# Attention, MLP and gate in one program: the middle of the run follows a written-out order table

## The chip, the core and the metric

The program runs on one core of a Trainium2 chip. Five engines work side by side, each through its own queue of instructions in order: PE (TensorE, matrix products into PSUM), ACT (ScalarE, activations), DVE (VectorE), POOL (GpSimd) and SP (SyncE, here only starting transfers). PSUM has eight banks of 128x512 fp32; a matrix product writes a bank and ScalarE or VectorE must have read it before it is written again. Between engines a semaphore carries "this is done"; inside an engine the order of the queue is all there is.

The metric is the device time of one execution in microseconds (us). Three runs of the kernel before gave 664.42, 664.42 and 664.57.

## What is computed

The input is x (2048 rows of 512), with 32 query heads of width 16 over one shared key and value head, and an MLP of width 1792. Cut to what matters:

```
xn = layernorm(x)
q  = (xn @ wq) as 32 heads of 16;  k = xn @ wk;  v = xn @ wv
p  = softmax(q k^T / 4);  s = (p v, heads side by side) @ wo
g  = silu( silu(xn @ w1) @ w2 )
out = x + s * g
```

All tensors are bf16 outside of PSUM.

## The kernel before

**Planning.** The program isn't written down instruction by instruction. While it is built, a planner (class `Planner`, from L117 on) keeps a clock for each engine and a price for each kind of work (`T_P` for a VectorE pass, `T_P64` for a GpSimd shift, `MM` for a group of matmuls and so on, L36 to L55). The main loop at the end of the kernel takes the engine whose clock is furthest behind and lets its step function (`pe_step`, `act_step`, `generic_step`) place one more operation: an instruction, or a group of four matmuls. What comes out is one list for each engine; `finalize` adds the semaphore waits that the reads and writes of tiles need. The clocks only settle the order. On the chip nothing is left of them.

**Scores.** Work is cut into 32 passes (`NG`), each of which has 512 queries of four heads (i = 0 to 3), and every head has 16 blocks of 128 keys. One product of 128 keys x 16 dimensions by 512 queries fills one PSUM bank (L946). It uses a strip of 32 of PE's rows, so up to four of them, on four strips and into four banks, run at once: an S group (`do_S`, L1086 on). Two engines turn scores into exponentials:

- ScalarE's way ("a"): one `Exp` activation over one, two or three neighbouring banks into `pa_sb` (`act_step`, L1845).
- VectorE's way ("d"): `tensor_scalar` multiplies by 128 log2(e), adds a constant and writes uint16, which read as bf16 is a rough 2^x, into `db_sb` (L1082). Four of those form a batch. GpSimd then adds 32, 64 and 96 to all values of a batch, as packed 64-bit sums, into `ds_sb` (the shifts, L1291; `make_shifts`, `split`): the same exponentials at other places of the rounding pattern. The four versions with weights `SHIFT_W` average its error away. A shift can also be done by VectorE (L1285).

Both ways need PE again: the product with v is 32 columns wide, so four run at once on column strips, one for each head, and add up in bank 7: a C group (`do_pv`, L1371). A key block of ScalarE's way needs one such product, one of VectorE's way four (one from `db_sb`, three from `ds_sb`). Columns of ones in `v_sb` give the sums of the softmax in the same products.

**Other work on PE.** Jobs (`mk_q`, `mk_h`, `mk_z`, `mk_w`) are the projections and the MLP: some rounds each, a round being a C group (L577), with a bank of their own from start to eviction. A round can also be cut into four pieces of 32 rows (`piece`, L689); a piece fits into the free strip of an S group that has three score products. Job results go through ScalarE (`Tanh`, L740) and VectorE (L742), or VectorE alone (L699, L796).

**Normalisation.** When a pass is done, VectorE transposes bank 7 (L1427), takes reciprocals (L1430), multiplies (L1431, `otr_sb`) and, every second pass, transposes again (L1438).

**Who excludes whom.** Some VectorE instructions have two inputs in tiles, or read and write tiles only: `otr_sb` (L1431), `ob_sb` (L808), the shift on VectorE (L1285). The planner marks them with `ports=2`, as it does GpSimd's shifts, and never lets one of VectorE's and one of GpSimd's run at the same time: `place` makes each wait by semaphore for the last marked operation of the other engine (`last2`), and `avail` keeps a shift back if a marked VectorE task will be ready within `HOLD_PO`.

**What sets the order around the change.** `pe_step` chooses between an S group, a group with v and a job round by thresholds on queues and banks; `do_S` chooses how many products go which way and into which banks; `act_step` takes up to three finished scores in neighbouring banks; `generic_step` takes VectorE's and GpSimd's ready task of the best priority. Random numbers with fixed seeds (`SEEDS`, `redraw`, `vary`) vary these choices every eight S groups. The start (load, layer norm, first keys: the first `NPRO` jobs) and the end (`make_tail`: the last product with wo, the gate and the stores) have code of their own.

Of the kernel before, what the change touches and what calls it, by code (L numbers as in the profile page):

```python
# [15 lines left out]
P = 128  # L16
DH = 16
NQ = 512
# [31 lines left out]
K = len(SHIFT)  # L50
PH = []

PE, AC, DV, PO, SP = "PE", "ACT", "DVE", "POOL", "SP"
ENGINES = (PE, AC, DV, PO, SP)
MM = 216.0  # L55
BLG = 0
# [38 lines left out]


class Task:
    __slots__ = ("eng", "dur", "emit", "reads", "writes", "prio", "preds", "op", "on_place", "dma", "gate", "ports", "after", "ring", "first")

    def __init__(self, eng, dur, emit, reads=(), writes=(), prio=5, preds=(), on_place=None, dma=0, gate=None, ports=1):  # L100
        self.ports, self.after, self.ring = ports, None, None
# [210 lines left out]
def bass_recurrent_scan__grouped_kv_mqa__dense_activation_silu__prompt_kernel(  # L312
# [30 lines left out]
    with ExitStack() as es:  # L343
# [350 lines left out]
        def mk_q(oi):  # L694
            c, o = divmod(oi, NOC)

            def consume(jb, op):
                b = jb.bank
                t = Task(DV, T_P, lambda v: v.tensor_scalar(qt_sb[:, oi % NQR, :], bank(b), QSCALE, None, op0=ALU.mult),  # L699
                         [("ps", b)], [("qT", oi % NQR)], 0)  # L700
                q_done[oi] = t
# [31 lines left out]
        def gated(b, k, scale, dst, key, kind):  # L733
            src, held = bank(b), ("ps", b)
            t0 = None
            if kind in EVAC:
                src, held = hs_sb[:, k, :], ("hs", k)
                t0 = Task(DV, T_P, lambda v: v.tensor_copy(hs_sb[:, k, :], bank(b)), [("ps", b)], [held], 0,
                          [hs_last.get(k)])
            t1 = Task(AC, 490.0, lambda a: a.activation(t_sb[:, k, :], src, ACT.Tanh, scale=scale),  # L740
                      [held], [("t", k)], 0, [t0])
# [3 lines left out]
            t2.first = [t1, t2] if t0 is None else [t0]  # L745
            if t0 is not None:
                hs_last[k] = t2
                pl.add(t1)
                pl.add(t2)
            return t2  # L750
# [54 lines left out]
        def final(tt, b, r=None):  # L805
            t1 = scaled(tt, b, r)
            src, key = fin_of(tt, r)
            t2 = Task(DV, 333.0, lambda v: v.tensor_tensor(ob_sb[:, tt % 4, :], src, xr_sb[:, tt % 4, :], ALU.add),  # L808
                      [key, ("xr", tt % 4)], [("ob", tt % 4)], PR_OB if r is None else 1,
                      [t1, xr_task[tt], out_task.get(tt - 4)], ports=2)  # L810
            fin_task[tt], out_task[tt] = t2, store(tt, t2)
            return t1, t2

# [261 lines left out]
        def pass_d(b, bt, g, i, kt):  # L1075
            tot[g, i] += K

            def placed(pop):
                pool_free.append(b)
                pvq[g][i].append((pop, v_lhs(1, g, kt), db_sb[:, bt.b, i * NQ:(i + 1) * NQ].bitcast(BF16),  # L1080
                                  [("Db", bt.b, i)] + v_reads(1, kt), ("d", bt), None))
            bt.P[i] = pl.add(Task(DV, T_P, lambda v: v.tensor_scalar(  # L1082
                db_sb[:, bt.b, i * NQ:(i + 1) * NQ], bank(b), 128.0 * LOG2E, 128.0 * (SHIFT_BETA + 127.0),
                op0=ALU.mult, op1=ALU.add), [("ps", b)], [("Db", bt.b, i)], 0, on_place=placed))

        def do_S(t):  # L1086
            banks = [b for r, b in bank_times() if r <= t + 30][:4]
# [328 lines left out]
        def make_norm(g):  # L1416
# [6 lines left out]
            if g == NG - 1:  # L1423
# [9 lines left out]
                rcp_sb[:, k, :].unsqueeze(2).to_broadcast([P, NQ // 32, DH]), ALU.mult),  # L1433
                [("F", k), ("rcp", k)], [("otr", oi % 2, e)], PR_OTR, [t2, t2_task.get(oi - 2)], ports=2))
            norm[("m", g)] = t3
            if e == 1:
                cc = oi // NOC - NON // NOC
                t2_task[oi] = pl.add(Task(DV, T_TR, lambda v: v.transpose(on_sb[:, oi % NON, :], otr_sb[:, oi % 2, :]),  # L1438
                                          [("otr", oi % 2, 0), ("otr", oi % 2, 1)], [("on", oi % NON)], 4,
                                          [t3, norm[("m", g - 1)]],  # L1440
                                          gate=lambda: cc < 0 or all(tt in w_rounds for tt in range(4 * cc, 4 * cc + 4))))


        kt1 = {}
# [334 lines left out]
        def half_step(t):  # L1779
# [24 lines left out]
                st["halfdone"] = True  # L1804
            return True

        def act_step():
            t = pl.clk[AC]
            now, soon = pl.best(AC, t)
# [29 lines left out]
                pl.place_task(now[1])  # L1839
                return True  # L1840
            if rx is not None and rx <= t + 25:
                q.sort(key=lambda u: u.bank)
                b0, b1 = q[0].bank, q[-1].bank
                step = q[1].bank - b0 if n > 1 else 1
                op = pl.place(AC, 0.8333 * NQ * n + T_AF, lambda a: a.activation(  # L1845
                    pa_sb[:, s * NQ:(s + n) * NQ].rearrange("p (b n) -> p b n", n=NQ), ps3[:, b0:b1 + 1:step, :], ACT.Exp),
                    [("ps", u.bank) for u in q], [("pA", s + d) for d in range(n)])
                for d in range(n):
                    pa_busy[s + d] = 1
                st["expn"] += n  # L1850
                for k, u in enumerate(q):
                    g, i, kt = u.slot
                    pool_free.append(u.bank)
                    pvq[g][i].append((op, v_lhs(0, g, kt), pa_sb[:, (s + k) * NQ:(s + k + 1) * NQ],
                                      [("pA", s + k)] + v_reads(0, kt), ("a", s + k), None))
                return True
            if soon is not None:
                nxt = min(nxt, soon[2])
            if rx is not None:
# [3 lines left out]
        def generic_step(e):  # L1863
            t = pl.clk[e]
            now, soon = pl.best(e, t)
            if now is not None:
                pl.place_task(now[1])
                return True
            return soon[2] if soon is not None else INF

        steps = {PE: pe_step, AC: act_step, DV: lambda: generic_step(DV), PO: lambda: generic_step(PO),
                 SP: lambda: generic_step(SP)}
        idle = {e: -1.0 for e in ENGINES}
        while True:
            e = min(ENGINES, key=lambda e: pl.clk[e])
# [73 lines left out]
```

## Time and profile before

| | |
|---|---|
| median of three runs | 664.42 us |
| span of the profiled execution | 662.9 us |
| time around the span (median less span) | 1.5 us |
| PE, ScalarE, VectorE, GpSimd busy | 652.8, 652.0, 613.6, 564.8 us |
| score products / products with v | 2048 / 4272 |
| exponential activations of ScalarE | 689, and 4 over half-width pairs of banks at the end |
| exponential passes of VectorE | 740 |
| shifts on GpSimd / on VectorE | 548 / 7 |

The profile is of one execution, with start and length of each instruction. Lengths include the time until the result has landed, so instructions of one engine overlap in it: the step from one start to the next is shorter than the length, and it is the step that says how much an engine can do. Groups of instructions are named by the line of the kernel, the engine, the operation and the tiles (out<-in). An idle time stands with the instruction that ended it (releaser).

### The profile page before, as it was taken

What the parts mean: (1) busy time and instruction counts of PE and PEld (TensorE: products, weight loads), DVE (VectorE), ACT (ScalarE), POOL (GpSimd) and SP (SyncE); (2) the same over time, 40 slices, a digit from 0 to 9 for tenths busy, and PEclk for the clock granted to TensorE, in tenths of its full rate; (3) what the DMA queues carried; (4) which work ended last, traced back from release to release, by engine and by line L of the source; (5) the groups of instructions that cost most, each with busy time, mean ns of one, the idle gap of its engine ahead of it and who ended that gap; (6) DMA issues with size and microseconds to landing.
All of it is one profiled execution on the core that took longest, in us unless ns stands there. A gap on an engine that the chain in (4) does not pass through costs nothing.

```text
span 662.9 us, 21201 instructions
## 1 busy us (share of the span) xinstructions
PE 652.8 (98%) x8958; PEld 189.3 (29%) x8959; DVE 613.6 (93%) x1085; ACT 652.0 (98%) x786; POOL 564.8 (85%) x564
## 2 busy tenths in 40 slices
PE   8899999999999999999999999999999999999997
PEld 4332222222222222222222222222222222222222
DVE  8989999999999999999999999999999999998986
ACT  7999999999999999999999999999999999999996
POOL 3059999999997889998999889899999888979973
PEclk9999999999999999999999999999999999999999
DMA  9500000000000100000000000000000001000000
GB/s 303 167 9 2 2 2 2 2 2 2 1 2 18 34 18 2 1 2 2 2 2 1 18 18 18 18 2 1 2 2 2 2 18 33 2 18 2 2 2 33
DMA packets 11501, 12.86 MB, mean 19 GB/s; under 512 B 1808, under 2 KB 10768, under 8 KB 11408
## 3 DMA queue, kind: packets, MB, share of 16 engines
q1 hardware_dynamic: 10784, 10.65, 5.0%
q8 instruction: 72, 1.18, 0.8%
q0 software_dynamic: 192, 0.46, 0.2%
q10 hardware_dynamic: 432, 0.39, 0.2%
q14 instruction: 21, 0.17, 0.1%
HBM read 8.95 MB, written 2.10 MB: 17 GB/s over the span
## 4 chain that ended last, share of the span: by engine, by line
PE 90%; ACT 4%; DVE 4%; DMA 1%; issue 0%; SPq 0%; DVEq 0%
PE ps L1371 40%; PE ps L946 30%; PE ps L577 19%; ACT pa_sb L1845 4%; DMA ds_sb<-in_A_x_dram 1%; DVE stats_sb L488 1%; DVE db_sb L1082 1%; ACT t_sb L740 0%; PE ps L593 0%; SPq L423 0%; DVE xn_sb L520 0%; DVE ds_sb L1285 0%; DVE xnT_sb L606 0%; DVE fin_sb L796 0%; DVE f_sb L1395 0%
## 5 line engine op out<-in xcount | busy, mean ns | idle before, releaser
L1845 ACT ACTIVATE pa_sb<-ps 128x1024 bf16<-128x1024 f32 (+2 forms) x689 | 615.4, 1004 | 2.9 <-PE ps L946 2.0
L1291 POOL INT64_ADD ds_sb<-db_sb x548 | 556.8, 1038 | 57.9 <-DVE otr_sb L1431 31.6
L1082 DVE TENSOR_SCALAR db_sb<-ps 128x512 uint16<-128x512 f32 x740 | 476.4, 682 | 35.5 <-PE ps L946 20.6
L1371 PE MATMUL ps<-ds_sb,v_sb 128*32 128x512 bf16 x2220 | 265.2, 384 | 0.2 <-DVE ds_sb L1285 0.2
L946 PE MATMUL ps<-qt_sb,kt_sb 32*128 32x512 bf16 x2048 | 250.3, 385 | 3.7 <-ACT pa_sb L1845 1.5
L1371 PE MATMUL ps<-pa_sb,v_sb 128*32 128x512 bf16 x1312 | 231.6, 383 | 0.2 <-DVE var_sb L512 0.2
L1371 PE MATMUL ps<-db_sb,v_sb 128*32 128x512 bf16 x740 | 161.6, 384 | 0.0
L946 PEld LDWEIGHTS ps<-qt_sb,kt_sb 32*128 32x128 bf16 x2048 | 62.7, 91 | 274.6 <-ACT pa_sb L1845 149.7
L1371 PEld LDWEIGHTS ps<-ds_sb,v_sb 128*32 128x32 bf16 x2220 | 63.8, 95 | 62.1 <-issue 45.2
L577 PE MATMUL ps<-xnT_sb,w_sb 128*32 128x512 bf16 x896 | 71.1, 383 | 0.0
L1371 PEld LDWEIGHTS ps<-pa_sb,v_sb 128*32 128x32 bf16 x1312 | 57.0, 95 | 43.3 <-issue 31.0
L577 PE MATMUL ps<-w_sb,u_sb 128*32 128x512 bf16 x776 | 62.5, 383 | 0.0
L689 PE MATMUL ps<-w_sb,u_sb 32*128 32x512 bf16 x120 | 46.2, 385 | 0.0
L1371 PEld LDWEIGHTS ps<-db_sb,v_sb 128*32 128x32 bf16 x740 | 40.0, 95 | 20.2 <-issue 15.4
L740 ACT ACTIVATE t_sb<-ps 128x512 bf16<-128x512 f32 x72 | 45.1, 626 | 0.0
L742 DVE SCALAR_TENSOR_TENSOR u_sb<-t_sb,ps 128x512 bf16<-128x512 bf16 x56 | 38.2, 683 | 1.1 <-ACT t_sb L740 0.2
L577 PEld LDWEIGHTS ps<-xnT_sb,w_sb 128*32 128x32 bf16 x896 | 18.2, 95 | 24.1 <-issue 16.1
L1427 DVE STREAM_TRANSPOSE f_sb<-ps 128x512 f32<-128x512 f32 x31 | 21.9, 706 | 1.9 <-PE ps L1371 1.8
L1448 POOL DMA_DIRECT2D kt_sb<-kt_sb x4 | 2.3, 563 | 24.9 <-DVE kt_sb L638 14.7
L577 PEld LDWEIGHTS ps<-w_sb,u_sb 128*32 128x32 bf16 x776 | 15.4, 95 | 19.9 <-issue 17.0
L577 PE MATMUL ps<-wo_sb,on_sb 128*32 128x512 bf16 x256 | 19.3, 383 | 0.0
L577 PE MATMUL ps<-xnT_sb,wq_sb 128*32 128x512 bf16 x240 | 18.7, 383 | 0.0
(83 smaller groups left out, 180.9 us busy)
## 6 DMA issues: line engine op xcount, KB each, us to landing
w_sb<-in_B_w_dram SPq DMA_DIRECT2D x2, 1792.0 KB, 14.0
xr_sb<-in_A_x_dram SPq DMA_DIRECT2D x16, 128.0 KB, 2.4
out_dram<-ob_sb SPq DMA_DIRECT2D x15, 128.0 KB, 1.7
ds_sb<-in_A_x_dram SPq DMA_DIRECT2D x3, 512.0 KB, 6.9
wq_sb<-in_A_wq_dram SPq DMA_DIRECT2D x1, 512.0 KB, 5.0
wo_sb<-in_A_wo_dram SPq DMA_DIRECT2D x1, 512.0 KB, 16.3
kt_sb<-kt_sb POOLq DMA_DIRECT2D x4, 112.0 KB, 3.8
ds_sb<-in_A_x_dram SPq DMA_DIRECT2D x2, 128.0 KB, 2.8
```

What stands on the lines that cost most here:

```text
L488: ts_ = pl.add(Task(DV, 593.0, lambda v, t=t: v.bn_stats(stats_sb[:, t, :], x_tile(t)), [xkey(t)], [("st", t)], 1 + j, gate=(lambda j=j: S ...
L577: last = h.matmul(bank(b)[32 * j:32 * (j + 1), 0:n], lhsT=lhs(j), rhs=rhs, start=start, stop=stop, tile_position=(0, 32 * j), skip_group_c ...
L689: return (lambda pe: pe.matmul(bank(b), lhsT=lhs(k, rows, 0, P), rhs=rhs(k, rows), start=False, stop=last, tile_position=(32 * i, 0), skip ...
L740: t1 = Task(AC, 490.0, lambda a: a.activation(t_sb[:, k, :], src, ACT.Tanh, scale=scale), [held], [("t", k)], 0, [t0])
L742: t2 = Task(DV, T_P, lambda v: v.scalar_tensor_tensor(out=dst, in0=t_sb[:, k, :], scalar=1.0, in1=src, op0=ALU.add, op1=ALU.mult), [held, ...
L946: return pe.matmul(bank(b), lhsT=kt_sb[32 * i:32 * i + 32, g % 2, kt * P:(kt + 1) * P], rhs=qt_sb[32 * i:32 * i + 32, (g // 2) % NQR, :], ...
L1082: bt.P[i] = pl.add(Task(DV, T_P, lambda v: v.tensor_scalar(db_sb[:, bt.b, i * NQ:(i + 1) * NQ], bank(b), 128.0 * LOG2E, 128.0 * (SHIFT_BET ...
L1291: whole["po"].append(pl.add(Task(PO, T_P64, lambda g, cols=cols: g.int64_add(ds_sb[:, s, cols].bitcast(U64), db_sb[:, bt.b, cols].bitcast( ...
L1371: h = pe.matmul(bank(OB)[32 * i:32 * (i + 1), cols], lhsT=lhs, rhs=rhs, start=s0, stop=s1, tile_position=(0, 32 * i), skip_group_check=True)
L1427: t1 = pl.add(Task(DV, T_TR, lambda v: v.transpose(f_sb[:, k, :], bank(OB)), [("ps", OB)], [("F", k)], 1, [norm.get(("m", g - 2))]))
L1448: kt1[c] = pl.add(Task(PO, T_SWDGE, lambda e: e.dma_start(kt_sb[DH:P, 1, cols], kt_sb[0:P - DH, 0, cols]), [("kt0", k) for k in range(4 * ...
L1845: op = pl.place(AC, 0.8333 * NQ * n + T_AF, lambda a: a.activation(pa_sb[:, s * NQ:(s + n) * NQ].rearrange("p (b n) -> p b n", n=NQ), ps3[ ...
```

## The change

The choices of `pe_step`, `act_step` and `generic_step` in the middle of the run are replaced by a table, `ORDER`, which has one string for each of PE, ScalarE, VectorE and GpSimd. It begins to hold when the jobs of the start are placed and no task of theirs is left (`ordered`), and each engine goes back to its own step function when its string is used up. The strings read like this:

- PE: `S` is an S group: how many products go ScalarE's way, how many VectorE's, a character for each that names bank and head, and a strip for a job piece or `.`. `L` adds one product to the S group just placed, on a free strip. `P` is a group with v, with a letter for each head: `a`, `d` or `s` for the tile it takes (`pa_sb`, `db_sb`, `ds_sb`) or `-`. `N` starts a job in the bank given, `J` is a job's next round.
- ScalarE: a digit is an exponential over so many banks, `T` a Tanh.
- VectorE: a digit is the eviction of that bank into `db_sb`; letters are q, the gate's product, the steps of the normalisation and the last steps of an output (tags given to the tasks).
- GpSimd: the place in its list of waiting shifts, always the first.

Two prices of the planner change too: `T_P` from 600 to 598 and `T_P64` from 1035 to 1014. `place_exp` is the old code of `act_step`, moved into a function. Activations still read only neighbouring banks.

```diff
-T_P, T_SH, T_TR, T_AF = 600.0, 600.0, 630.0, 64.3
-T_P64, DV_MIN, T_LIB = 1035.0, 40, 300.0
+T_P, T_SH, T_TR, T_AF = 598.0, 600.0, 630.0, 64.3
+T_P64, DV_MIN, T_LIB = 1014.0, 40, 300.0
...
+S_WIDE = 3.0
+ORDER = {
+    PE: (
+        "S216CM.LdfPaaaaN0JS11Yu.LaNJJPaaaaS214Al.LdyPaddaS21N[,.PdaaaPssadS214Bk.N6JJJS21M[..PaassS21:Dm.PssssPssaaPa-ssS01-.S21"
...
+    AC: (
+        "1122222T22222T2T222221T2T22222222222T2T12222222322232221T221T222222T2T2222222322222222222222T22323232222222222222T222222"
...
+    DV: (
+        "356Q56050H506a262bHc6H54656156H1H45645645645646a6H1H5Q25265265b6c5d252H5465H6256256a5Hb6cH2623623635625625625656a56b5c6d"
...
+        def ordered():
+            if not at.get("on"):
+                at["on"] = st["pro"] >= NPRO and not active and x_free[0] and not any(pl.tasks[e] for e in (AC, DV, PO)) and (
+                    pl.clk[PE] <= min(pl.clk[e] for e in (AC, DV, PO)))
+            return at["on"]
...
+        def order_S(late):
+            if late:
+                nA, nD, codes, gap = (1, 0, next_of(PE, 3)[2], ".") if next_of(PE, 2)[1] == "a" else (0, 1, next_of(PE, 3)[2], ".")
+                size = 3
+            else:
+                nA, nD = int(next_of(PE, 2)[1]), int(next_of(PE, 3)[2])
+                size = 4 + nA + nD
+                codes, gap = next_of(PE, size)[3:-1], next_of(PE, size)[-1]
+            slots = [slot_of(ch, k >= nA) for k, ch in enumerate(codes)]
+            if any(b not in pool_free for b, _, _ in slots):
+                return INF
...
+            dur = MM + (S_WIDE if len(mm) + (pj is not None) > 3 else 0.0)
+            start = pl.order[PE][-1].t0 + 10.0 if late else pe_start(pl.clk[PE], "S")
+            op = pl.place(PE, dur, emit, sorted(set(reads), key=str), writes,
+                          t0=max(start, pl.ready(PE, reads, writes)), after=pj.prev if pj is not None else None)
...
+        def order_task(e, tag):
+            task = next((x for x in pl.tasks[e] if x.tag == tag), None)
+            if task is None or pl.avail(task) is None:
+                return INF
+            at[e] += 1
+            pl.place_task(task)
+            return True
+
+        def order_step(e):
+            if e == PE:
+                return order_pe()
+            c = next_of(e)
+            if e == PO:
+                if len(pl.tasks[PO]) <= int(c) or pl.avail(pl.tasks[PO][int(c)]) is None:
+                    return INF
+                at[e] += 1
+                pl.place_task(pl.tasks[PO][int(c)])
+                return True
+            if e == DV or c == "T":
+                return order_task(e, c)
+            n = int(c)
+            if len(units) - st["expn"] < n or place_exp(units[st["expn"]:st["expn"] + n], pl.clk[AC]) is None:
+                return INF
+            at[e] += 1
+            return True
+
+        def step_of(e, own):
+            def step():
+                if ORDER and e in ORDER and ordered() and at[e] < len(ORDER[e]):
+                    return order_step(e)
+                return own()
+            return step
+
         steps = {PE: pe_step, AC: act_step, DV: lambda: generic_step(DV), PO: lambda: generic_step(PO),
                  SP: lambda: generic_step(SP)}
+        steps = {e: step_of(e, fn) for e, fn in steps.items()}
```

`order_pe` (not shown) reads the next letter and calls `order_S`, or places the group with v or the job round that the letter names.

More of the change, by code (lines that the diff above doesn't have):

```diff
@@ L1805, in half_step, with place_exp @@
             return True
+        def place_exp(q, t):
+            n = len(q)
+            free = [k for k in range(NPA - n + 1) if not any(pa_busy[k:k + n])]
+            if not free:
+                return None
+            s = min(free, key=lambda k: max(pl.ready(AC, (), [("pA", k + d)]) for d in range(n)))
+            q = sorted(q, key=lambda u: u.bank)
+            b0, b1 = q[0].bank, q[-1].bank
+            step = q[1].bank - b0 if n > 1 else 1
+            op = pl.place(AC, 0.8333 * NQ * n + T_AF, lambda a: a.activation(
+                pa_sb[:, s * NQ:(s + n) * NQ].rearrange("p (b n) -> p b n", n=NQ), ps3[:, b0:b1 + 1:step, :], ACT.Exp),
+                [("ps", u.bank) for u in q], [("pA", s + d) for d in range(n)])
+            for d in range(n):
+                pa_busy[s + d] = 1
+            st["expn"] += n
+            for k, u in enumerate(q):
+                g, i, kt = u.slot
+                pool_free.append(u.bank)
+                pvq[g][i].append((op, v_lhs(0, g, kt), pa_sb[:, (s + k) * NQ:(s + k + 1) * NQ],
+                                  [("pA", s + k)] + v_reads(0, kt), ("a", s + k), None))
+            return True
         def act_step():
@@ L1841, in act_step @@
             if rx is not None and rx <= t + 25:
[L1842 to L1856, printed above, removed]
+                return place_exp(q, t)
             if soon is not None:
```

222 lines of the change are left out of this document (220 added, 2 removed).

## The prediction

> **What bounds the kernel now.** I read the page first: the busy shares, then the shares of the chain that ended last.
>
> ```profile
> span 662.9 us, 21201 instructions
> PE 652.8 (98%) x8958; PEld 189.3 (29%) x8959; DVE 613.6 (93%) x1085; ACT 652.0 (98%) x786; POOL 564.8 (85%) x564
> PE 90%; ACT 4%; DVE 4%; DMA 1%; issue 0%; SPq 0%; DVEq 0%
> ```
>
> Four engines are nearly full, but the chain lies on PE for 90%. A busy share can't say how full PE is, since a matmul's record is longer than the step to the next. The pieces of that chain, in order of time, give the price of PE's work (start, length, what):
>
> ```profile
> 644.95 1.19 PE ps L1371 x20
> 646.14 0.33 PE ps L946 x4
> 646.47 0.98 PE ps L1371 x16
> ```
>
> Matmuls go in groups of four that run at once, in two kinds: S groups (score products on row strips, L946, with a 32-row piece of a job, L689, in a free strip) and C groups (column strips: L1371, L577). Five C groups take 1.19 and four 0.98, so a C group costs 0.21 to 0.22 (0.216 below; the last digit is from start times); four cost 0.86, so 0.11 is left for the change of kind, and an S group lasts 0.33, 0.11 over a C group, for the change back. A pair of changes costs 0.22.
>
> The timeline of PE shows the same step by step, and the only waits in it (start, length, instruction):
>
> ```profile
> 61.36 0.60 PE L577 MATMUL ps<-xnT_sb,w_sb 128*32 128x512 bf16 x8
> 61.94 0.39 PE L946 MATMUL ps<-qt_sb,kt_sb 32*128 32x512 bf16 x3
> ...
> 302.37 0.39 PE L946 MATMUL ps<-qt_sb,kt_sb 32*128 32x512 bf16 x3
> 302.38 0.38 PE L689 MATMUL ps<-w_sb,u_sb 32*128 32x512 bf16 x1
> 302.70 0.62 PE L1371 MATMUL ps<-ds_sb,v_sb 128*32 128x512 bf16 x8
> 303.25 0.39 PE L946 MATMUL ps<-qt_sb,kt_sb 32*128 32x512 bf16 x3
> ...
> 637.66 0.62 PE L1371 MATMUL ps<-ds_sb,v_sb 128*32 128x512 bf16 x8
> 638.26 0.39 PE L946 MATMUL ps<-qt_sb,kt_sb 32*128 32x512 bf16 x3
> ...
> 636.92 1.88 DVE L1082 TENSOR_SCALAR db_sb<-ps 128x512 uint16<-128x512 f32 x3
> ```
>
> From 302.37 to 303.25 is one turn: 3 groups of 0.216 and 0.22 of changes are 0.87. The S group after the C groups of 302.70 starts 0.55 later, the one after those of 637.66 starts 0.60 later: it waited 0.05. Of the 587 S groups between 60 and 640, 69 start over 0.02 late like this (first and last: 61.94 and 638.26), 4.6 us in all, and each starts some 0.06 after a VectorE eviction ended. In the last row three of these run 0.60 apart, (1.88 - 0.68)/2, 0.68 each: the second ends at 638.20, and the S group follows at 638.26. The last bank wanted was VectorE's. C groups are never late there. So PE sets the end: its groups and changes, and 4.6 us of waits.
>
> **The change part by part.** I counted in the order of the two built programs. The first 501 matmuls, 112 VectorE and 55 ScalarE instructions and the last 49 matmuls are the same; the order between is new.
>
> *PE.* S groups fall from 638 to 618: 2048 score products stay, the job pieces beside them rise from 120 to 132, and in 61 places a score product is appended late to a standing group (code L). C groups rise from 1616 to 1621: 16 more key blocks go through VectorE's exponential, four products instead of one, +48 matmuls; the 12 pieces take 3 rounds off, and 4 more go because fewer groups stand part empty. Groups: -15 x 0.216 = -3.2. Runs of S groups between C groups fall from 638 to 616: -22 x 0.22 = -4.8. Together -8.1 us on the bounding engine.
>
> A late product (L) is an operation that before does not have. At least it costs what the piece in the rows above costs, 0.01 (302.37 to 302.38); at most a C group's 0.22, if it ran after the others. It uses a free strip as the piece does, but has a bank of its own to wait for, so I take 0.02: +1.2 us; the ends are 0.6 and 13.4.
>
> *ScalarE.*
>
> ```profile
> L1845 ACT ACTIVATE pa_sb<-ps 128x1024 bf16<-128x1024 f32 x593 | 562.5, 1050 | 1.3 <-PE ps L946 0.6 <-PE ps L689 0.2
> L1845 ACT ACTIVATE pa_sb<-ps 128x512 bf16<-128x512 f32 x85 | 48.2, 624 | 1.6 <-PE ps L946 1.5
> L1845 ACT ACTIVATE pa_sb<-ps 128x1536 bf16<-128x1536 f32 x11 | 16.1, 1485 | 0.0
> ...
> 217.94 0.62 ACT L740 ACTIVATE t_sb<-ps 128x512 bf16<-128x512 f32 x1
> 218.42 1.06 ACT L1845 ACTIVATE pa_sb<-ps 128x1024 bf16<-128x1024 f32 x1
> ...
> 298.20 4.69 ACT L1845 ACTIVATE pa_sb<-ps 128x1024 bf16<-128x1024 f32 x5
> ```
>
> Exponentials over two banks go from 593 to 559, over one from 85 to 53, over three from 11 to 39. From start to start two banks cost (4.69 - 1.05)/4 = 0.91, one 0.48 (217.94 to 218.42), three 0.91 + (1.485 - 1.050) = 1.345. So -34 x 0.91 - 32 x 0.48 + 28 x 1.345 = -8.6 us. ScalarE's work falls as far as PE's; it hides behind PE as before (the idle column: 1.3 and 1.6 us) and adds nothing to the sum. Without that cover PE's -8.1 would be capped at this -8.6: no difference.
>
> The Trainium skill (ScalarE: Activation LUTs, What ACT_TABLE_LOAD costs) gives an ACTIVATE 186 ns + 0.833 ns an element and an overlap of 93 ns back to back. That makes 1039 ns for two banks alone, which the row's 1050 bears out, but 946 from start to start, where the trace has 910; by it, as an estimate, ScalarE would save 10.4 us, and before would need 658 us on ScalarE, more than the trace has room for.
>
> *VectorE and GpSimd.*
>
> ```profile
> L1291 POOL INT64_ADD ds_sb<-db_sb x548 | 556.8, 1038 | 57.9 <-DVE otr_sb L1431 31.6 <-DVE ob_sb L808 13.0 <-PE ps L1371 5.5
> L1285 DVE TENSOR_SCALAR ds_sb<-db_sb 128x2048 uint16<-128x2048 uint16 x7 | 4.4, 687 | 0.1
> ...
> DVE db_sb L1082 <- PE ps L946: 20.6, 82, 0.8
> DVE db_sb L1082 <- PE ps L689: 8.5, 40, 0.4
> DVE otr_sb L1431 <- POOL ds_sb L1291: 0.7, 1, 0.7
> ...
> POOL ds_sb L1291 <- DVE otr_sb L1431: 31.6, 30, 1.7
> POOL ds_sb L1291 <- DVE ob_sb L808: 13.0, 11, 1.5
> ...
> 40.51 3.06 POOL L1291 INT64_ADD ds_sb<-db_sb  x3 [3.90 <-DVE db_sb L1082]
> 645.25 6.11 POOL L1291 INT64_ADD ds_sb<-db_sb  x6 [3.34 <-DVE ds_sb L1285]
> ...
> 654.70 0.29 PE L1371 MATMUL ps<-pa_sb,v_sb 128*32 128x256 bf16 x2
> ```
>
> VectorE gets 16 more evictions at 0.60 and gives up its 7 shifts of about 0.6: +5.4 us. GpSimd gets 19 shifts more: 556.8 x 567/548 = 576.1, +19.3 us. Neither is on PE's chain, but both lose their room. GpSimd's shifts run from 40.5 to 651.4. In 41 places it stands still until a VectorE instruction with two tile inputs (otr_sb or ob_sb) is done, 44.6 us in all; VectorE almost never waits the other way (0.7). The last shift must be done 8.4 before the end (8.2 from the first half-width group at 654.70, and one C group more that now stands behind it). If the span becomes 657.5, GpSimd can stand still 657.5 - 8.4 - 40.5 - 576.1 = 32.5 us. The other 12.1 must go over to VectorE, which then waits for GpSimd, and the evictions queued behind it keep PE's banks. VectorE's own room is the 29.1 us it waited for PE: less 5.4 of work and 5.4 of shorter span, 18.3; less 12.1, 6 are left.
>
> So the 4.6 us of late S groups should grow. Bounds: all gone, -4.6; all 12.1 landing on PE, +12.1. Most handovers have room on one side or the other, as 41 of them cost PE little before, so I stay near the measured 4.6 and add a third: +1.5.
>
> *Moved and unchanged.* The order of SP's transfers and of the four that GpSimd issues is the same, and no queue is passed. T_P, T_P64 and the order table exist while the program is built; the chip runs none of it: 0. The last z job's 14 rounds move behind the last S group; they fill the time of the last three shifts, now on GpSimd (3 x 1.02 against 3 x 0.6). If that cover failed, 3 x 0.4 = 1.2 us would show at the end.
>
> *Sum.* -8.1 + 1.2 + 1.5 = -5.4 on the profiled span of 662.9, which is 657.5. The median of the runs, 664.4, lies 1.5 above that span, for what is around it: 659.0.
>
> **The rivals.**
>
> *The room is used up, no change.* The saved 8.1 comes back as late S groups, VectorE having 6 us of room left in the whole run. For it: every late start of before was VectorE's. Against: the late starts were short, 0.07 on average. Price: waits up by about 6, late products 1.2: 664.4 - 8.1 + 7.2 = 663.5.
>
> *GpSimd becomes the bound, slower.* If GpSimd keeps losing 44.6 us in the handovers, its last shift ends at 40.5 + 576.1 + 44.6 = 661.2, the span at 669.6 and the time at 671.1. It decides from the point where its standstill passes 662.9 - 8.4 - 40.5 - 576.1 = 37.9 us; a standstill between gives 665 to 671. For it: 19 more shifts on an engine that lost 1.1 us at each handover. Against: between the VectorE instruction that feeds the shift ahead of a handover and the handover itself now stand 4 to 15 VectorE instructions, median 8, before 6 to 20, median 12; VectorE comes to the handover sooner, which shortens GpSimd's part. The Trainium skill (SBUF — State Buffer, Who interferes with whom) says that a VectorE instruction with two SBUF inputs and a GpSimd instruction that reads SBUF exclude each other, and the second blocks until the first is done. By that rule an order can only choose which side waits; the 41 waits agree.
>
> *More than the sum.* A wider look-ahead could also remove the waits: 664.4 - 8.1 + 0.6 - 4.6 = 652.3. For it: all of them come from one kind of dependency. Against: VectorE has less room to do it with.
>
> That the order isn't followed is excluded: the counts above are of the built program.
>
> **How the numbers follow.** Forecast, 655 to 663: 0.66. No change, 663 to 665.7: 0.11. GpSimd bound: 0.17. More than the sum, under 655: 0.06. A difference under 0.2% (1.3 us) can't be told from none here. Faster (under 663.1): 0.66 + 0.06 + a little of the second case, 0.74. Same: 0.09. Slower: 0.17. The range 654.5 to 666.5 leaves out most of the third case and part of the fourth, about 0.2; the forecast's own range is 655 to 663.
>
> **What would show it.** Right: S groups 618 in PE's timeline with turns of the same 0.87; ScalarE's two-bank exponentials still 0.91 apart in runs; GpSimd's idle time before shifts near 33 us, and new waits of otr_sb on GpSimd, some 12 us, in VectorE's list. Wrong: late S groups over 10 us in all, L products that push the next C group by 0.1 or more, or a last shift that ends later than 649. GpSimd's standstill above 38 us would make the time slower than before.

## The result, and the profile after

The changed kernel takes 658.09 us, the median of 4 runs (657.81 to 658.24), against 664.47 (664.42 to 664.57) before on the same chip: a ratio of 0.9903, 95% interval 0.9889 to 0.9917. The profiled span fell from 662.9 to 656.3. Line numbers are higher after the change: S groups are L1068, PV products L1494, rounds of jobs L696, job pieces L808, evictions L1204, shifts L1414, otr_sb L1554, ob_sb L929, exponentials L1941.

The page of the changed kernel, span, busy shares and shares of the chain:

```profile
span 656.3 us, 21267 instructions
PE 646.6 (99%) x9007; PEld 199.4 (30%) x9007; DVE 614.7 (94%) x1094; ACT 642.2 (98%) x748; POOL 585.0 (89%) x583
PE 92%; POOL 3%; DVE 3%; DMA 1%; ACT 1%; SPq 0%; issue 0%; DVEq 0%
```

PE's share of the chain is 92% where it was 90; ScalarE's fell from 4 to 1, VectorE's from 4 to 3, and GpSimd appears with 3. Pieces of that chain in order of time (start, length, what):

```profile
616.95 0.33 PE ps L1068 x4
617.28 0.76 PE ps L1494 x12
618.04 0.57 PE ps L1068 x4
618.61 0.76 PE ps L1494 x12
...
643.62 3.02 PE ps L696 x56
```

Three C groups cost 0.76 and the S group of 616.95 costs 0.33, as before. The S group of 618.04 costs 0.57, for its fourth matmul is a late product (L). The timelines of PE and of VectorE at that place (the chain's times lie 0.07 later than the starts here):

```profile
614.71 0.39 PE L1068 MATMUL ps<-qt_sb,kt_sb 32*128 32x512 bf16 x3
...
615.03 0.61 PE L696 MATMUL ps<-w_sb,u_sb 128*32 128x512 bf16 x8
615.58 0.39 PE L1068 MATMUL ps<-qt_sb,kt_sb 32*128 32x512 bf16 x3
...
617.97 0.64 PE L1068 MATMUL ps<-qt_sb,kt_sb 32*128 32x512 bf16 x4
618.54 0.39 PE L1494 MATMUL ps<-ds_sb,v_sb 128*32 128x512 bf16 x2
```

```profile
616.88 0.69 DVE L862 SCALAR_TENSOR_TENSOR tmp_sb<-t_sb,ps 128x512 bf16<-128x512 bf16 x1
617.48 0.68 DVE L1204 TENSOR_SCALAR db_sb<-ps 128x512 uint16<-128x512 f32 x1
```

A turn of one S and two C groups is 0.87 as it was (614.71 to 615.58). At 617.97 four matmuls take 0.64 instead of 0.39 from the first start to the last end, so the last began 0.25 later, at 618.22. VectorE's eviction ended at 617.48 + 0.68 = 618.16: the product started 0.06 after the bank that it writes was free.

The groups of shifts and exponentials, then the waits of GpSimd and of VectorE (total, times, longest):

```profile
L1414 POOL INT64_ADD ds_sb<-db_sb x567 | 577.0, 1040 | 33.9 <-DVE otr_sb L1554 19.0 <-DVE ob_sb L929 8.8 <-DVE db_sb L1204 5.4
L1941 ACT ACTIVATE pa_sb<-ps 128x1024 bf16<-128x1024 f32 x559 | 529.1, 1051 | 1.1 <-PE ps L1068 0.9
```

```profile
DVE db_sb L1204 <- PE ps L1068: 12.7, 33, 0.9
...
DVE db_sb L1204 <- PE ps L808: 4.7, 22, 0.4
...
DVE otr_sb L1554 <- POOL ds_sb L1414: 1.5, 4, 0.8
...
POOL ds_sb L1414 <- DVE otr_sb L1554: 19.0, 28, 1.6
...
POOL ds_sb L1414 <- DVE ob_sb L929: 8.8, 12, 1.0
```

GpSimd stood still at handovers for 19.0 + 8.8 = 27.8 us in 40 places, before 44.6 in 41, and VectorE hardly waits for it more than it did (1.5 against 0.7). The first and the last stretch of shifts in GpSimd's timeline:

```profile
39.26 6.11 POOL L1414 INT64_ADD ds_sb<-db_sb  x6 [2.91 <-DVE db_sb L1204]
...
632.07 15.26 POOL L1414 INT64_ADD ds_sb<-db_sb  x15 [1.38 <-DVE otr_sb L1554]
```

The last shift ends at 647.3. From 39.26 to there lie 608.1 us, of which 577.0 are shifts and 31.0 standstill (33.9 less the 2.9 before the first). From the last shift to the end of the span are 9.0 us, where the prediction wanted at least 8.4.

Of the S groups between 60 and 640 us, 34 started over 0.02 late in the trace, 2.6 us in all; before 69, 4.6 us. Before, the bank that came free last was VectorE's each time; now it is VectorE's in 19 of the 34 (1.7 us) and ScalarE's in 15 (0.8).

### The profile page after: what moved, and what is told of

Read it like the earlier page. It is cut to its first block, busy times and chain, and to the rows that moved or that the text cites. A ratio compares the mean times of both kernels' runs of the same rounds, so it can differ in the third digit from the quotient of the medians.

```text
span 656.3 us, 21267 instructions
## 1 busy us (share of the span) xinstructions
PE 646.6 (99%) x9007; PEld 199.4 (30%) x9007; DVE 614.7 (94%) x1094; ACT 642.2 (98%) x748; POOL 585.0 (89%) x583
## 4 chain that ended last, share of the span: by engine, by line
PE 92%; POOL 3%; DVE 3%; DMA 1%; ACT 1%; SPq 0%; issue 0%; DVEq 0%
PE ps L1494 42%; PE ps L1068 30%; PE ps L696 19%; POOL ds_sb L1414 3%; DMA ds_sb<-in_A_x_dram 1%; DVE stats_sb L607 1%; ACT pa_sb L1941 1%; PE ps L712 0%; SPq L542 0%; DVE xn_sb L639 0%; DVE kt_sb L757 0%; DVE u_sb L862 0%; DVE xnT_sb L725 0%; DVE v_sb L782 0%; PE ps L743 0%
## 5 line engine op out<-in xcount | busy, mean ns | idle before, releaser
L1414 POOL INT64_ADD ds_sb<-db_sb x567 | 577.0, 1040 | 33.9 <-DVE otr_sb L1554 19.0
L1941 ACT ACTIVATE pa_sb<-ps 128x1024 bf16<-128x1024 f32 (+2 forms) x651 | 604.4, 1040 | 2.7 <-PE ps L1068 2.2
L1204 DVE TENSOR_SCALAR db_sb<-ps 128x512 uint16<-128x512 f32 x756 | 481.3, 682 | 23.4 <-PE ps L1068 12.7
L1494 PE MATMUL ps<-ds_sb,v_sb 128*32 128x512 bf16 x2268 | 287.8, 383 | 0.0
L1068 PE MATMUL ps<-qt_sb,kt_sb 32*128 32x512 bf16 x2048 | 246.1, 384 | 3.4 <-ACT pa_sb L1941 1.3
L1494 PE MATMUL ps<-pa_sb,v_sb 128*32 128x512 bf16 x1296 | 246.4, 383 | 0.0
L1494 PE MATMUL ps<-db_sb,v_sb 128*32 128x512 bf16 x756 | 185.6, 383 | 0.0
L1068 PEld LDWEIGHTS ps<-qt_sb,kt_sb 32*128 32x128 bf16 x2048 | 64.3, 90 | 252.5 <-ACT pa_sb L1941 155.4
L1494 PEld LDWEIGHTS ps<-ds_sb,v_sb 128*32 128x32 bf16 x2268 | 71.6, 95 | 68.4 <-issue 48.9
L1494 PEld LDWEIGHTS ps<-pa_sb,v_sb 128*32 128x32 bf16 x1296 | 60.6, 95 | 38.7 <-issue 28.1
L696 PE MATMUL ps<-xnT_sb,w_sb 128*32 128x512 bf16 x876 | 62.9, 382 | 0.0
L696 PE MATMUL ps<-w_sb,u_sb 128*32 128x512 bf16 x796 | 60.4, 383 | 0.0
L1494 PEld LDWEIGHTS ps<-db_sb,v_sb 128*32 128x32 bf16 x756 | 45.9, 95 | 22.8 <-issue 15.2
L808 PE MATMUL ps<-w_sb,u_sb 32*128 32x512 bf16 x100 | 38.5, 384 | 0.0
L696 PEld LDWEIGHTS ps<-xnT_sb,w_sb 128*32 128x32 bf16 x876 | 19.1, 95 | 23.4 <-DVE db_sb L1204 6.0
L696 PEld LDWEIGHTS ps<-w_sb,u_sb 128*32 128x32 bf16 x796 | 15.7, 95 | 22.2 <-issue 15.0
L696 PE MATMUL ps<-wo_sb,on_sb 128*32 128x512 bf16 x256 | 18.6, 382 | 0.0
L696 PE MATMUL ps<-xnT_sb,wq_sb 128*32 128x512 bf16 x228 | 17.0, 382 | 0.0
```

The lines of the kernel that those rows point to most:

```text
L696: last = h.matmul(bank(b)[32 * j:32 * (j + 1), 0:n], lhsT=lhs(j), rhs=rhs, start=start, stop=stop, tile_position=(0, 32 * j), skip_group_c ...
L808: return (lambda pe: pe.matmul(bank(b), lhsT=lhs(k, rows, 0, P), rhs=rhs(k, rows), start=False, stop=last, tile_position=(32 * i, 0), skip ...
L1068: return pe.matmul(bank(b), lhsT=kt_sb[32 * i:32 * i + 32, g % 2, kt * P:(kt + 1) * P], rhs=qt_sb[32 * i:32 * i + 32, (g // 2) % NQR, :], ...
L1204: bt.P[i] = pl.add(Task(DV, T_P, lambda v: v.tensor_scalar(db_sb[:, bt.b, i * NQ:(i + 1) * NQ], bank(b), 128.0 * LOG2E, 128.0 * (SHIFT_BET ...
L1414: whole["po"].append(pl.add(Task(PO, T_P64, lambda g, cols=cols: g.int64_add(ds_sb[:, s, cols].bitcast(U64), db_sb[:, bt.b, cols].bitcast( ...
L1494: h = pe.matmul(bank(OB)[32 * i:32 * (i + 1), cols], lhsT=lhs, rhs=rhs, start=s0, stop=s1, tile_position=(0, 32 * i), skip_group_check=True)
```

## The experiments

| kernel | median us | ratio to the kernel before, 95% interval | against 658.1 |
|---|---|---|---|
| prices of before, with the table | 665.42 | 1.0016 (1.0007 to 1.0025) | +7.3 |
| prices of before, handover places of the change | 658.34 | 0.9907 (0.9892 to 0.9922) | +0.2 |
| new prices, no table | 670.68 | 1.0095 (1.0078 to 1.0112) | +12.6 |
| table to the half | 666.32 | 1.0030 (1.0018 to 1.0042) | +8.2 |
| 39 C groups more | 665.93 | 1.0021 (1.0011 to 1.0031) | +7.8 |
| 39 groups of the S kind more | 671.46 | 1.0103 (1.0088 to 1.0119) | +13.4 |
| ScalarE 9 us more | 667.57 | 1.0049 (1.0034 to 1.0064) | +9.5 |
| ScalarE 8 us less | 657.93 | 0.9901 (0.9886 to 0.9916) | -0.2 |
| GpSimd 8 us more | 663.89 | 0.9989 (0.9980 to 0.9998) | +5.8 |
| GpSimd 17 us more | 670.97 | 1.0097 (1.0082 to 1.0112) | +12.9 |
| GpSimd 11 us less | 657.80 | 0.9900 (0.9885 to 0.9915) | -0.3 |
| VectorE 8 us more | 660.35 | 0.9939 (0.9922 to 0.9955) | +2.3 |

The last column is the difference to the changed kernel. The kernel before, run beside each of these, had medians from 664.35 to 664.58, so 0.2 or 0.3 in the last column is no difference. The second, eighth, eleventh and twelfth rows were run after the other eight.

### The prices of before, with the table

```diff
-T_P, T_SH, T_TR, T_AF = 598.0, 600.0, 630.0, 64.3
-T_P64, DV_MIN, T_LIB = 1014.0, 40, 300.0
+T_P, T_SH, T_TR, T_AF = 600.0, 600.0, 630.0, 64.3
+T_P64, DV_MIN, T_LIB = 1035.0, 40, 300.0
```

> The changed kernel with the two prices T_P and T_P64 set back to 600 and 1035; the order table stays. The instructions' order is then the same on every engine, and 18 of PE's groups use another bank. Theory (PE's groups and changes of kind set the end, and the table alone makes their number): 658, between 657 and 659.5. Rival (the prices, which decide banks and so waits, are part of the gain): above 661.

Measured 665.42: the theory missed by over 7 us, and the whole gain is gone. Waits and timelines of this kernel:

```profile
POOL ds_sb L1414 <- DVE otr_sb L1554: 24.8, 28, 1.6
...
POOL ds_sb L1414 <- DVE ob_sb L929: 11.9, 12, 2.0
...
PE ps L1494 <- POOL ds_sb L1414: 4.3, 11, 0.6
```

```profile
452.93 0.40 PE L1494 MATMUL ps<-ds_sb,v_sb 128*32 128x512 bf16 x4
453.77 0.39 PE L1494 MATMUL ps<-ds_sb,v_sb 128*32 128x512 bf16 x1 [0.45 <-POOL ds_sb L1414]
...
639.28 15.24 POOL L1414 INT64_ADD ds_sb<-db_sb  x15 [1.30 <-DVE otr_sb L1554]
```

A kind of wait appears that neither kernel had: a C group whose shifted tile isn't there yet. The one of 453.77 starts 0.84 after the one ahead of it, where 0.22 is due. By the trace's start times 16 C groups behind C groups are late like this between 60 and 640, 5.6 us in all (after the change none, before one of 0.06). GpSimd stands still at the same 40 handovers for 36.7 us instead of 27.8, and its last shift ends at 654.5.

The planner keeps VectorE's instructions with two tile inputs and GpSimd's shifts apart by a dependency in the program: whichever of the two is placed second waits for the other. The order on either engine doesn't say which is second; the planned clocks do, and with them the prices. Between the two programs each engine's order is the same but for some rounds of wo in the tail (which bank or which buffer of a tile an instruction uses differs in places), but in 36 of 69 places the two-input instruction is put one to three shifts earlier in GpSimd's row when a shift is priced at 1035 instead of 1014. GpSimd then arrives at the handover sooner than VectorE and stands.

### The prices of before, with the handover places of the change

```diff
+def hand(pl):
+    two = {e: [op for op in pl.order[e] if op.ports == 2] for e in (DV, PO)}
...
+    for op, n in zip(two[DV], GIVE):
+        if n:
+            op.deps.append(two[PO][n - 1])
+    for k, op in enumerate(two[PO]):
+        n = sum(g <= k for g in GIVE)
+        if n:
+            op.deps.append(two[DV][n - 1])
```

GIVE holds, for each of the 69 instructions, how many shifts go ahead of it in the changed kernel.

> The kernel with the two prices set back (665.4), and in it alone the places of the handovers between VectorE's two-input instructions and GpSimd's shifts as in the changed kernel: which shift waits for which of them and the other way round, 36 of 69 differ, by one to three shifts. Both engines' orders stay as they are. Theory (the prices work through these places: with 600 and 1035 the plan puts the handovers one to three shifts too early in GpSimd's row, and it stands still there): 658 to 659.5. Rival (the prices work through something else, as the eight rounds of wo that stand elsewhere in the tail): 664 to 666.

Measured 658.34. GpSimd's waits are back at the changed kernel's, and PE's list has none on GpSimd:

```profile
POOL ds_sb L1431 <- DVE otr_sb L1571: 19.7, 28, 1.6
...
POOL ds_sb L1431 <- DVE ob_sb L946: 8.4, 11, 1.0
```

This kernel keeps the other banks, buffers and wo rounds of the kernel with the prices of before, so the 7.3 us are the handover places, and nothing else that the prices decide.

### The new prices without the table

```diff
-ORDER = {
...
-}
+ORDER = {}
```

> The changed kernel with an empty order table: the new prices alone, with the choice at each place made as in before. Counted in the built program: 639 S groups (before 638), 1683 C groups (before 1667, with the prologue), 639 runs of S (before 638), no late products. Theory (PE's groups and changes): 17 x 0.216 + 0.22 = 3.9 over before, 668 (665 to 670). Rival (completion pace and banks make the gain, by fewer waits, whatever the groups' number): 658 to 662.

Measured 670.68, 0.7 over the theory's range and far from the rival's. The groups are worth 3.9 by count; late S groups rose from 4.6 to 8.5 us (108 of them), which with the groups is more than the 6.2 measured against before. The table is needed, and the prices alone do harm.

### The table to the half

```diff
-                if ORDER and e in ORDER and ordered() and at[e] < len(ORDER[e]):
+                if ORDER and e in ORDER and ordered() and at[PE] < len(ORDER[PE]) // 2 and at[e] < len(ORDER[e]):
```

> The table obeyed until half of PE's string is used, the choices of before from there. Counted in the built program: 629 S groups, 1684 C groups, 625 runs of S, 32 late products. Theory (PE's groups and changes): against before 8 x 0.216 - 13 x 0.22 = -1.1, and about 1 for late products: 664 (662 to 665.5). Rival (the gain is in waits and spreads evenly over time): half of it, 661. Rival (only the table's last part pays, at the tail): 664 too, but then with the first half's stages as long as before; by the theory the first 300 us gain some 3.3 us on before.

Measured 666.32, 0.8 over the range; the split of the time agrees. The 1024th of the 2048 score products starts at 333.5 us before, at 330.0 here and at 330.4 in the changed kernel: the first half gains 3.5, forecast 3.3. The 1920th starts at 612.8, 614.4 and 604.4: the gain is lost again once the choices of before go on from the table's state, with 54.2 us of GpSimd's idle time before shifts. Against the changed kernel the count says +6.1 (19 groups, 9 pairs of changes), the late S groups +2.0 (4.6 against 2.6) and the late products, fewer here, -1.6 (2.1 against 3.7, reckoned as further down): 6.5 of the 8.2 measured. The other 1.7 was not placed.

### C groups and changes of kind added

At 39 of the PV groups:

```diff
+                if idle:
+                    for i in range(4):
+                        pe.matmul(bank(OB)[32 * i:32 * (i + 1), :], lhsT=zer_sb[:, 32 * i:32 * (i + 1)], rhs=zer_sb[:, :],
+                                  start=False, stop=False, tile_position=(0, 32 * i), skip_group_check=True)
```

> In the changed kernel, 39 C groups more: after each 24th group of PV products four more matmuls on column strips, which add zero products to the same bank. No further change of kind. Theory (PE sets the end): 39 x 0.216 = 8.4 us more, less what late starts and late products give back (6 us in all, of which a part): 663 to 666.5. Rival (ScalarE, 98% busy, sets the end as much): under 660.

Measured 665.93, +7.8 of 8.4. In the other kernel one matmul on a 32-row strip takes their place:

```diff
+                if idle:
+                    pe.matmul(bank(OB), lhsT=zer_sb[0:32, 0:P], rhs=zer_sb[0:32, :],
+                              start=False, stop=False, tile_position=(0, 0), skip_group_check=True)
```

> At the same 39 places one zero matmul on a 32-row strip, the kind of the S groups, instead of the four on column strips: a group and a pair of changes of kind more in each. Theory (a group 0.216, a pair of changes 0.22): 39 x 0.436 = 17.0 us more than the changed kernel, 671 to 675, and 8.6 more than with the 39 C groups. Rival (a change of kind costs nothing by itself, and the 0.11 steps around S groups are a matter of the banks waited for): the same time as with the 39 C groups, within 1.5.

Measured 671.46, +13.4. The matmul stands ahead of its PV group, and in 9 of the 39 places an S group comes right before it, so no pair of changes is added there; in 3 of the 9 it starts together with that S group, on a free strip, and adds no group either. The sum is 30 x 0.436 + 6 x 0.216 = 14.4, not the 17.0 expected. In the timeline the matmul starts 0.33 after the group ahead and 0.32 before the next:

```profile
313.02 0.39 PE L1500 MATMUL ps<-db_sb,v_sb 128*32 128x512 bf16 x1
...
313.35 0.39 PE L1497 MATMUL ps<-zer_sb 32*128 32x512 bf16 x1
313.67 0.39 PE L1500 MATMUL ps<-pa_sb,v_sb 128*32 128x512 bf16 x2
```

Beside the kernel with 39 C groups this one has 30 pairs of changes more and 3 groups less: 671.46 - 665.93 = 5.5, and 3 x 0.216 on top, make 6.2, or 0.21 a pair. The rival, no price for a change, falls. The Trainium skill (TensorEngine Tiling (Array Packing), Key Properties) says that a change of the tiling mode drains TensorE, without a price; the 0.10 more at each side of this matmul agrees with it. Some 1.0 us less than the sum came through; the late S groups fell from 2.6 to 1.8 us, which is most of it.

### ScalarE: 9 us more, 8 us less

```diff
+def _cut(ch):
+    _n[0] += ch == "2"
+    return "11" if ch == "2" and _n[0] % 3 == 0 else ch
+
+
+ORDER[AC] = "".join(_cut(ch) for ch in ORDER[AC])
```

> In the changed kernel every third exponential over two banks is replaced by two over one bank: 183 places, each 2 x 0.477 - 0.904 = 0.05 more, +9 us of ScalarE's work, which undoes the 8.6 us that the change took off it; PE's order stays. Theory (ScalarE's saving hides behind PE): 658 to 661, since banks come free earlier with the smaller pieces and later with the sum. Rival (the saved ScalarE time is the gain): 666 to 667.

Measured 667.57, +9.5: the theory missed, all of the added work came through. (The pieces are smaller too, which moves the times at which banks come free; more work and smaller pieces aren't told apart here.) The timelines of PE and ScalarE show how:

```profile
560.58 1.04 PE L705 MATMUL ps<-wo_sb,on_sb 128*32 128x512 bf16 x16
561.74 0.40 PE L1077 MATMUL ps<-qt_sb,kt_sb 32*128 32x512 bf16 x4
...
558.60 3.08 ACT L1950 ACTIVATE pa_sb<-ps 128x1024 bf16<-128x1024 f32 x4
```

Four C groups from 560.58 and a change of kind, 0.97, make an S group due at 561.55. It starts at 561.74, 0.06 after an exponential ended at 561.68. By start times 122 S groups are late here, 10.9 us in all, where the changed kernel has 34 and 2.6: 8.3 of the 9.5 us. In 92 of the 122, 8.1 us, the bank that came free last was ScalarE's.

```diff
+            wide = NQ if st["expn"] < 100 else NQ - 8
...
-                pa_sb[:, s * NQ:(s + n) * NQ].rearrange("p (b n) -> p b n", n=NQ), ps3[:, b0:b1 + 1:step, :], ACT.Exp),
+                pa_sb[:, s * NQ:(s + n) * NQ].rearrange("p (b n) -> p b n", n=NQ)[:, :, 0:wide], ps3[:, b0:b1 + 1:step, 0:wide], ACT.Exp),
```

> In the changed kernel each exponential on ScalarE after the first 100 banks covers 504 of 512 columns; the other 8 keep what was there. 1188 banks, 0.0067 us each, about 7.9 us less work. Theory (PE sets the end, ScalarE is only full): 656 to 658.5. Rival (ScalarE is the bound, as the 9.5 us for 9 us of added work could be read): 649 to 651.

Measured 657.93, -0.2: the rival falls. ScalarE is full, but it isn't what sets the end. Its groups and the busy shares of this kernel's page:

```profile
L1942 ACT ACTIVATE pa_sb<-ps 128x1008 bf16<-128x1008 f32 x525 | 493.0, 1025 | 1.9 <-PE ps L1068 1.0
```

```profile
PE 647.0 (99%) x9007; PEld 200.5 (31%) x9007; DVE 615.0 (94%) x1094; ACT 640.7 (98%) x748; POOL 584.0 (89%) x583
```

### GpSimd: 8 and 17 us more, 11 us less

```diff
+        old, new = pl.order[PO], []
+        for n, o in enumerate(old):
+            new.append(o)
+            if n >= 60 and n % 40 == 0 and n < len(old) - 20:
+                op = Op()
+                op.eng, op.emit, op.deps, op.inc, op.val, op.know, op.sem, op.ports = PO, lambda g: g.memset(dum_sb[:], 0.0), [], False, 0, None, None, 1
...
+                new.append(op)
+        pl.order[PO][:] = new
```

The second kernel has n % 20 in place of n % 40.

> In the changed kernel 13 idle writes to a scratch tile in GpSimd's order, one after every 40 instructions, 0.68 us each by the tile's size, about 8.8 us in all. Theory (GpSimd has room: 33.9 us of standstill, of which about 11.5 could be made up): +0 to +2 on the changed kernel. Rival (GpSimd is now the bound): +7 to +9.

> The same idle writes after every 20 instructions, 27 of them, about 18.4 us. Theory (GpSimd's room ends at about 11.5 us): +5 to +9. Rival (GpSimd is the bound): +16 to +19. Rival (its standstill is made up in full before PE feels it): under +2.

The writes were 12 and 25. Their records are 0.74 us long, but by start times each pushes the next shift back by 0.68, as expected: 8.2 and 17.0 us. They cost 5.8 and 12.9, 71 and 76% of that: more than the theory gave in both, and not the rival's whole. In the first, late S groups rose from 2.6 to 7.1 us, 4.5 of the 5.8, and 6.2 of the 7.1 stand behind VectorE's banks. How it reaches PE, in the waits of the first and in its timelines:

```profile
DVE otr_sb L1555 <- POOL ds_sb L1415: 6.5, 13, 1.1
...
POOL ds_sb L1415 <- DVE otr_sb L1555: 17.7, 27, 1.5
```

```profile
207.54 0.38 PE L1495 MATMUL ps<-pa_sb,v_sb 128*32 128x512 bf16 x1
208.40 0.40 PE L1069 MATMUL ps<-qt_sb,kt_sb 32*128 32x512 bf16 x4 [0.48 <-DVE db_sb L1205]
...
206.38 0.43 DVE L1555 TENSOR_TENSOR otr_sb<-f_sb,rcp_sb 128x256 bf16<-128x256 f32 x1 [0.69 <-POOL ds_sb L1415]
206.72 0.42 DVE L930 TENSOR_TENSOR ob_sb<-fin_sb,xr_sb 128x512 bf16<-128x512 bf16 x1
207.06 1.28 DVE L1205 TENSOR_SCALAR db_sb<-ps 128x512 uint16<-128x512 f32 x2
```

GpSimd is late at a handover, VectorE's otr_sb waits 0.69 for it, the second of the evictions behind it ends at 208.34, and the S group that wants that bank starts 0.06 later, 0.54 after it was due (207.54 + 0.32).

```diff
+                nsh[0] += 1
+                wide = 512 if nsh[0] <= 60 else 500
...
-                    ds_sb[:, s, cols].bitcast(U64), db_sb[:, bt.b, cols].bitcast(U64), words),
+                    ds_sb[:, s, cols].bitcast(U64)[:, 0:wide], db_sb[:, bt.b, cols].bitcast(U64)[:, 0:wide], words),
```

> In the changed kernel each shift of GpSimd from the 61st on covers 500 of its 512 columns; the other 12 keep what was there. 507 shifts, about 12 us less work by share. Theory (PE's groups and changes set the end, GpSimd is only full): 656 to 658.5. Rival (GpSimd is the bound, as the 73% of the added idle writes that came through could be read): 12 x 0.73 = 8.7 less, 648 to 651.

Measured 657.80, -0.3: GpSimd isn't the bound either. Its work fell by 10.9 us (577.0 to 566.1) and its idle time before shifts rose by 10.2 (33.9 to 44.1):

```profile
L1418 POOL INT64_ADD ds_sb<-db_sb x567 | 566.1, 1020 | 44.1 <-DVE otr_sb L1558 24.3 <-DVE ob_sb L929 11.0 <-DVE db_sb L1204 6.7
```

### VectorE: 8 us more

The same idle writes in VectorE's order, after every 32 instructions:

```diff
+            if n >= 150 and n % 32 == 0 and n < len(old) - 20:
+                op = Op()
+                op.eng, op.emit, op.deps, op.inc, op.val, op.know, op.sem, op.ports = DV, lambda v: v.memset(dum_sb[:, 0:512], 0.0), [], False, 0, None, None, 1
```

> In the changed kernel 29 idle writes to a scratch tile in VectorE's order, one after every 32 instructions, some 0.3 to 0.55 us each, 9 to 16 us in all. Theory (VectorE has room, the 17 us that it waits for PE): under a third of it comes through, 659 to 662. Rival (the orders are woven so closely that no engine has room where it is needed): 70% and more of it, 665 to 670.

```profile
L2196 DVE MEMSET dum_sb<- 128x256 uint32 x29 | 7.9, 272 | 0.1
```

They took 7.9 us, below the estimate, and cost 2.3, or 29%: the theory. VectorE has room where the other three have little or none. The pieces are smaller than GpSimd's (0.27 against 0.68 each), so part of the difference to GpSimd may be their size; that wasn't tried.

## Why the prediction was right, and where its steps were not

**The bound.** PE sets the end. Work added to PE comes through at 93% (7.8 of 8.4, and 13.4 of 14.4), and 11 us taken from GpSimd or 8 from ScalarE bring 0.3 and 0.2. No run takes work off PE alone; that PE sets the end rests on its share of the chain and on these two signs together. The counts carry the gain: with the prices that the turn of 0.87 shows unchanged, -22 pairs of changes are -4.8 and the groups -2.6. The prediction has -3.2 for the groups, and 0.6 of that is a miscount: an S group ends where a strip is used a second time, and by that the built program has 621 of them and 58 products appended late, not 618 and 61. So it is -12 groups, not -15, and -7.4 together, not -8.1. The counts aren't enough by themselves: with the prices of before they are the same, and the gain is gone.

**Late products and late S groups.** Both were mis-sized, in opposite directions. For L the step "I take 0.02: +1.2 us" fell. The 573 runs of S groups between 60 and 640 last 4.6 us longer than as many single ones, from their start to the C group's; four whole S groups more than runs are 0.9 of it, so the 58 late products cost 3.7, or 0.06 each, inside the ends given (0.6 to 13.4). A late product waits for a bank, not for a strip: between 60 and 640, 47 of them start over 0.03 after their group, and 46 of the 47 start 0.06 after VectorE's eviction of the very bank ended, as in the rows shown, where the wait was 0.25. The late S groups were to grow by 1.5 and fell by 2.0: by these rows part of the waiting for VectorE moved from S groups to late products. The two together are 1.7 instead of 2.7. The sum -7.4 + 3.7 - 2.0 is -5.7; the span fell by 6.6, and the other 0.9 was not placed. That the forecast of -5.4 lies so near is in part luck: three terms were off by 0.7, 2.5 and -3.5, and cancel.

**ScalarE.** "It hides behind PE as before" and "adds nothing to the sum" hold as far as they go: 8 us less brings nothing. But the cover has no slack. With 9 us put back, in smaller pieces, the time is 667.6: the gain is gone, as the sentence on the lost cover had it, and 3 us more with it. ScalarE's saving was no part of the gain, but by this run the gain needs it.

**VectorE and GpSimd.** The allowed standstill was right: 32.5 forecast, 31.0 measured, with the last shift at 647.3 against the limit of 649. The step that failed is how GpSimd would get there: "The other 12.1 must go over to VectorE". The 29.1 us that VectorE waited for PE fell to 17.4 (12.7 and 4.7), as its room was used, but it waits for GpSimd only 1.5 at otr_sb, not some 12. The standstill at handovers fell by 16.8 without a counterpart, from 1.09 to 0.70 each. The Trainium skill (SBUF — State Buffer, Who interferes with whom) was read in the prediction as leaving an order only the choice of the side that waits. The runs show a third way, that both arrive nearly together: then VectorE loses next to nothing (1.5 us in 4 places), and GpSimd stands still for the instruction's own 0.42 and the passing on of the semaphores, 0.56 at the shortest and 0.62 in the middle one of the 40. The two are kept apart by the program's own waits in all these kernels, so no run here shows what the chip's exclusion would do by itself.

**The prices.** The step "T_P, T_P64 and the order table exist while the program is built; the chip runs none of it: 0" was wrong in its last figure, and this is the step that failed worst. Counts and orders are the table's, but the places of the handovers are the prices', worth 7.3 us with the table given: as much as the whole gain. The same working would have given the same 659.0 for the kernel with the prices of before, which takes 665.42; that the change had the better prices in it is luck as far as the prediction goes. The trace of before had the number that says so: six shifts take 6.11 with a last record of 1.04, so they start 1.014 apart. That is the price assumed now, and not the 1035 that the plan assumed.

**The rivals.** The slower one, GpSimd as the bound, was to decide from a standstill of 37.9 us. The kernel with the prices of before has the changed order and stands 38.7 (41.6 before shifts in all, less 2.9 before the first): its span is 664.0, 1.1 over that of before, and C groups wait 5.6 us there, by start times, for the most part for GpSimd's tiles. In this one kernel the rival's mechanism and its threshold agree with the measurement, and the handover places keep the change on the other side of it. "No change" and "more than the sum" did not occur.

**The tail.** The cover that the z rounds should give to the last three shifts held: they run for 3.02 us behind the last S group, and the shifts end at 647.3 without a wait of PE on GpSimd.

## What to carry to other kernels

When several engines are matched as closely as here, an engine off the critical path can be worth nothing if it is made faster and cost most or all of its price if it is made slower; test both signs before calling an engine free or bound. A planner's price is part of the program wherever it decides which of two engines goes first: compare the dependencies of two builds, not only each engine's order. Set such prices to the measured step (from start to start, not the record's length), and look for handovers at which one side stands far longer than the shortest one in the trace.

## What was not expected of the hardware

A busy share and a mean record of ScalarE say little of its room. With 8 columns a bank less, the records of two banks fell from 1051 to 1025 ns, but ScalarE's busy time only from 642.2 to 640.7: by start times the shortest step from one to the next fell from 0.904 to 0.890, and the mean step stayed at 0.924. The records overlap by some 0.15, and shorter waits than that lie hidden inside them. In the kernel with more pieces the same two-bank exponential has a longer record at the same shortest step:

```profile
L1950 ACT ACTIVATE pa_sb<-ps 128x1024 bf16<-128x1024 f32 x376 | 397.0, 1155 | 0.7 <-PE ps L1077 0.6
```
